# Chunk attention feeding a gated MLP on one core: heads on partition quadrants with runs of 6 or 12 tokens, block transposes in 4-byte words, v as fp32 through the hardware queues, short first blocks

## The chip, the cores and the metric

The program runs on one core of one Trainium2 chip. The metric is the device time of one execution in microseconds (us), and the median over runs is quoted. The profile is of one further execution, taken by the hardware profiler; its times count from the first instruction ("the span").

Engines are named as the profile names them: PE multiplies matrices (PEld is its weight load), DVE is the vector engine, ACT the scalar engine, POOL is GpSimd, SP only issues transfers. Each engine executes its instructions in the order in which the program gives them. Transfers issued from POOL go through the queue that the profile calls software_dynamic; in this kernel they turn fp32 in DRAM into fp16 on the chip on the way. Those issued from SP (and, after the change, from ACT) are called hardware_dynamic and keep the type. All of them pass the core's 16 DMA engines.

## The reference, cut to what matters

```python
# q, k, v: (8, 8, 576, 64) fp32 = batch, heads, sequence, head size
def _attn_ref(q, k, v):                    # chunks of 64 tokens, each attends to itself alone
    q_c = q.reshape(B, H, nc, 64, D)       # k_c and v_c likewise
    scores = scale * np.matmul(q_c, k_c.transpose(0, 1, 2, 4, 3))
    scores = scores - np.max(scores, axis=-1, keepdims=True)
    attn = np.exp(scores)
    attn = attn / (np.sum(attn, axis=-1, keepdims=True) + 1e-09)
    return np.matmul(attn, v_c).reshape(B, H, S, D)

def _moe_ref(x, w_in, w_out, beta):        # x: 4608 tokens x 512; w_in 512 x 2048; w_out 2048 x 512
    h = x @ w_in
    g = h * (1.0 / (1.0 + np.exp(-beta * h)))
    return (g @ w_out).astype(np.float32)

def reference(q, k, v, moe_w_in, moe_w_out, moe_beta):
    attn_out = _attn_ref(q, k, v)
    x = attn_out.transpose(0, 2, 1, 3).reshape(B * S, H * D)
    return _moe_ref(x, moe_w_in, moe_w_out, moe_beta)
```

## The kernel before, in words

All matrix work is in fp16 with fp32 sums. The weights stay on the chip (`w_in16`, `w_out16`). The 4608 tokens pass in 18 units of 256 tokens for the attention, and in 10 blocks for the MLP: two of one unit, then eight of two units (512 tokens).

The attention of a unit has two parts. `emit_sc` (L130) multiplies k by q for all 8 heads of four chunks, 64 small matmuls into two PSUM tiles `sc`, and takes exp on ACT into `et`. `emit_pv` (L149) works on 128 tokens: 16 matmuls of `et` with v and a column of ones give `x` and the row sums; DVE takes the reciprocal (L162) and scales into `x16` (L164); a DMA transpose issued from SP (L169) puts 128 tokens of `xt`, features on partitions, in place for the MLP.

q, k and v come through POOL's queue, converted to fp16 (L87, L95). A partition holds two neighbouring tokens of all heads, so a run of q or k in DRAM is 2 x 64 floats, 512 bytes, and one of v 64 floats, 256 bytes. `emit_T` (L117) then makes the head size the contracted dimension with four DVE transposes per unit in 32x32 blocks of fp16, 512 elements per partition each.

The MLP of a block has two parts. `emit_m(j, m)` (L175) computes 128 of the 2048 hidden features: 4 matmuls into `hps` (L181), tanh on ACT into `sg` (L189), and one DVE instruction for `(sg + 1) * hps` into `gt` (L190; the halves are in `beta2_sb` and in the last scaling). `emit_t(j, t)` (L194) multiplies 128 tokens of `gt` by `w_out16`, 16 matmuls (L197), copies on ACT (L205) and stores from SP (L207).

The order is written out by hand. POOL issues: unit 0, a quarter of w_in, unit 1, the other three quarters, unit 2, four quarters of w_out, unit 3. In block j, between `emit_m(j, 3)` and `emit_m(j, 4)`, stand up to four `emit_t` of block j - 1, each with a step of the attention (for block j + 1) ahead of it. A block's first `emit_m` needs all of its `xt`.

Of the kernel before, what the change touches and what calls it, by code (L numbers as in the profile page):

```python
# [6 lines left out]

FP32 = mybir.dt.float32
FP16 = mybir.dt.float16
ACTF = mybir.ActivationFunctionType  # L10
ALU = mybir.AluOpType
# [3 lines left out]
def kernel(  # L15
# [17 lines left out]
    UNIT = 256  # L33
    NU = NT // UNIT
    NTILE = NT // 128
    VP = 80
# [4 lines left out]
    qk_p = ctx.enter_context(tc.tile_pool(name="qk", bufs=5))  # L41
# [3 lines left out]
    x_p = ctx.enter_context(tc.tile_pool(name="x", bufs=3))  # L45
    gt_p = ctx.enter_context(tc.tile_pool(name="gt", bufs=2))
# [5 lines left out]

    beta_sb = const.tile([128, KFF], FP32)
# [3 lines left out]
    vbig = big.tile([128, NTILE, H, VP], FP16)  # L57

    blocks = []
    u0 = 0  # L60
    for n in [1, 1] + [2] * ((NU - 2) // 2):
        blocks.append((u0, n))
        u0 += n
    NB = len(blocks)
    xt_t = {}
    unit_block = {}
    for j, (u0, n) in enumerate(blocks):
        xt_t[j] = big.tile([128, KDM, n * UNIT], FP16, name=f"xt{j}")
        for u in range(u0, u0 + n):
            unit_block[u] = (j, u - u0)  # L70

    def runs(t0, n):
        done = 0
        while done < n:
            b, s = divmod(t0 + done, S)
            step = min(n - done, S - s)
            yield done, step, b, s
            done += step

    q_t = {}  # L80
    k_t = {}

    def load_qk(u):
        for src, dst, nm in ((q, q_t, "qu"), (k, k_t, "ku")):
            t = qk_p.tile([128, H, 2, D], FP16, tag=nm, name=nm)
            for off, n, b, s in runs(u * UNIT, UNIT):
                nc.gpsimd.dma_start(  # L87
                    out=t[off // 2:(off + n) // 2],
                    in_=src[b, :, s:s + n, :].rearrange("h (p r) d -> p h r d", r=2),
                )  # L90
            dst[u] = t

    def load_v(i):
        for off, n, b, s in runs(i * 128, 128):
            nc.gpsimd.dma_start(  # L95
                out=vbig[off:off + n, i, :, 0:D],
                in_=v[b, :, s:s + n, :].rearrange("h p d -> p h d"),
            )
# [18 lines left out]
    def emit_T(u):  # L117
        for src, dst, nm in ((k_t, kT, "kT"), (q_t, qT, "qT")):
            a = src.pop(u)
            t = qt_p.tile([128, H, 2, 32, 2], FP16, tag=nm, name=nm)  # L120
            for r in range(2):
                nc.vector.transpose(  # L122
                    out=t[:, :, :, :, r],
                    in_=a[:, :, r, :].rearrange("p h (e i) -> p h e i", e=2),
                )
            dst[u] = t

    et_t = {}

    def emit_sc(u):  # L130
        qt, kt = qT.pop(u), kT.pop(u)
        sc = [ps_s.tile([128, H, CH], FP32, tag=f"sc{s}", name=f"sc{s}") for s in range(2)]
        for h in range(H):
            for e in range(2):
                for c in range(4):
                    p0, o0 = 32 * c, 64 * (c % 2)
                    nc.tensor.matmul(  # L137
                        out=sc[c // 2][o0:o0 + 64, h, :],
                        lhsT=kt[p0:p0 + 32, h, e].rearrange("p i r -> p (i r)"),
                        rhs=qt[p0:p0 + 32, h, e].rearrange("p i r -> p (i r)"),  # L140
                        start=(e == 0),
                        stop=(e == 1),
                    )
        for s in range(2):
            et = et_p.tile([128, H, CH], FP16, tag=f"et{s}", name=f"et{s}")
            nc.scalar.activation(out=et, in_=sc[s], func=ACTF.Exp, scale=scale)
            et_t[u, s] = et

    def emit_pv(u, s):  # L149
        i = 2 * u + s  # L150
        et = et_t.pop((u, s))
        x = ps_x.tile([128, 2, 4, 128], FP32, tag="x", name="x")
        for h in range(H):
            for c in range(2):
                p0 = 64 * c
                nc.tensor.matmul(  # L156
                    out=x[p0:p0 + 64, h // 4, h % 4, 0:D + 1],
                    lhsT=et[p0:p0 + 64, h, :],
                    rhs=vbig[p0:p0 + 64, i, h, 0:D + 1],
                )  # L160
        rd = rd_p.tile([128, 2, 4, 1], FP32, tag="rd", name="rd")
        nc.vector.reciprocal(out=rd, in_=x[:, :, :, D:D + 1])  # L162
        x16 = x_p.tile([128, 2, 4, D], FP16, tag="x16", name="x16")
        nc.vector.tensor_tensor(  # L164
            out=x16, in0=x[:, :, :, 0:D], in1=rd.to_broadcast([128, 2, 4, D]), op=ALU.mult
        )
        j, o = unit_block[u]
        t0 = o * UNIT + s * 128
        nc.sync.dma_start_transpose(  # L169
            out=xt_t[j][:, :, t0:t0 + 128], in_=x16.rearrange("p a h d -> p (a h d)")  # L170
        )
# [3 lines left out]
    def emit_m(j, m):  # L175
        n = blocks[j][1] * UNIT
        if m == 0:
            gt_t[j] = gt_p.tile([128, KFF, n], FP16, tag="gt", name="gt")
        hps = ps_p.tile([128, n], FP32, tag="p", name="hps")
        for kk in range(KDM):  # L180
            nc.tensor.matmul(  # L181
                out=hps,
                lhsT=w_in16[:, kk, m * 128:(m + 1) * 128],
                rhs=xt_t[j][:, kk, :],
                start=(kk == 0),
                stop=(kk == KDM - 1),
            )
        sg = sg_p.tile([128, n], FP32, tag="sg", name="sg")
        nc.scalar.activation(out=sg, in_=hps, func=ACTF.Tanh, scale=beta2_sb[:, m:m + 1])  # L189
        nc.vector.scalar_tensor_tensor(  # L190
            out=gt_t[j][:, m, :], in0=sg, scalar=1.0, in1=hps, op0=ALU.add, op1=ALU.mult
        )

    def emit_t(j, t):  # L194
        ops = ps_p.tile([128, DM], FP32, tag="p", name="ops")
        for kk in range(KFF):
            nc.tensor.matmul(  # L197
                out=ops,
                lhsT=gt_t[j][:, kk, t * 128:(t + 1) * 128],
                rhs=w_out16[:, kk, :],  # L200
                start=(kk == 0),
                stop=(kk == KFF - 1),
            )
        osb = osb_p.tile([128, DM], FP32, tag="osb", name="osb")
        nc.scalar.activation(out=osb, in_=ops, func=ACTF.Copy, scale=0.5)  # L205
        r0 = blocks[j][0] * UNIT + t * 128
        nc.sync.dma_start(out=out[r0:r0 + 128, :], in_=osb)  # L207

    attn = [[("sc", 0)], [("pv", 0, 0)]]
    for u in range(NU):  # L210
        attn.append(([("sc", u + 1)] if u + 1 < NU else []) + [("pv", u, 1)])
        if u + 1 < NU:
            attn.append([("pv", u + 1, 0)])
    attn.reverse()
    nxt_T = [0]
    nxt_load = [0]

    def loads_to(u):
        while nxt_load[0] <= min(u, NU - 1):
            w = nxt_load[0]  # L220
            load_qk(w)
            load_v(2 * w)
            load_v(2 * w + 1)
            nxt_load[0] += 1

    def attn_step():
        if not attn:
            return
        for op in attn.pop():
            if op[0] == "sc":  # L230
                emit_sc(op[1])
                if op[1] + 1 < NU:
                    emit_T(op[1] + 1)
                loads_to(op[1] + 4)
            else:
                emit_pv(op[1], op[2])

    with tc.manual_schedule():
        nc.sync.dma_start(out=beta_sb, in_=moe_beta.rearrange("(k p) -> p k", p=128))
        nc.vector.memset(vbig[:, :, :, D:D + 1], 1.0)  # L240
        loads_to(0)
        load_w_in(0)
        loads_to(1)
# [3 lines left out]
        loads_to(2)  # L247
        load_w_out(0)
        load_w_out(1)
        load_w_out(2)  # L250
        load_w_out(3)
        loads_to(3)
        nc.scalar.activation(out=beta2_sb, in_=beta_sb, func=ACTF.Copy, scale=0.5)
        emit_T(0)
        for _ in range(3):
            attn_step()
        pend = []
        for j in range(NB):
            for m in range(KFF):
                if m == 4:  # L260
                    n_a = 4 if j else 2
                    for t in pend:
                        if n_a:
                            attn_step()
                            n_a -= 1
                        emit_t(j - 1, t)
                    pend = []
                if m in (4, 7, 10, 13) and n_a and (m > 4 or j == 0):
                    attn_step()
                    n_a -= 1  # L270
                emit_m(j, m)
            pend = list(range(2 * blocks[j][1]))
# [32 lines left out]
```

The softmax here doesn't subtract the row's maximum and nothing guards it: scores larger than these inputs give would overflow.

## Time and profile before

| | |
|---|---|
| median of 3 runs | 347.1 us (345.27 to 348.63) |
| the profiled execution's own time | 350.12 us |
| its span, first to last instruction | 348.3 us |
| PE busy | 288.9 us, 83% of the span |
| DVE, ACT, POOL busy | 175.7, 144.5, 77.2 us |
| mean granted TensorE clock | 0.968 |
| DMA through POOL's queue | 79360 packets, 18.36 MB |
| DMA through the hardware queues | 26832 packets, 14.17 MB |

Bytes are counted as written, so a packet of q, k, v or weights counts half of what it read. In the page, busy time and clock stand in 40 slices of the span; the chain that ended last is followed back from the last instruction, step by step, to what released it. Waits are given as "who waited for whom". Where PE is busy in nearly all of a stretch, this stretch is PE's; where it isn't, the chain names what it waited for.

### The profile page before, as it was taken

How to read it: one execution, taken by the hardware profiler on the slowest of the kernel's cores; microseconds unless marked ns; L12 is line 12 of the kernel's file. 1: busy time of each engine (PE TensorE's matmuls, PEld its weight loads, DVE VectorE, ACT ScalarE, POOL GpSimd, SP SyncE). 2: the span in 40 equal slices, each digit the busy share in tenths (PEclk: the TensorE clock that was granted, in tenths of full speed). 3: DMA queues.
4: the chain of work that ended last, by engine and by line, in shares of the span. 5: the costliest groups of instructions: out<-in, count | busy, mean ns of one | idle time of the engine just before them, and what ended most of it. 6: DMA issues, size and time to landing. Idle time of an engine off the chain costs nothing.

```text
span 348.3 us, 7008 instructions
## 1 busy us (share of the span) xinstructions
PE 288.9 (83%) x2944; PEld 142.9 (41%) x2944; DVE 175.7 (50%) x305; ACT 144.5 (41%) x234; POOL 77.2 (22%) x100
## 2 busy tenths in 40 slices
PE   0110274983998599999999999999999999999995
PEld 0110263561443245445544444444444444444442
DVE  1413083662649264685377468637745822720700
ACT  1110153361357222752573275257427623732711
POOL 8628286803053035005402100000000000000000
PEclk9999997896799899999999999999999999999999
DMA  9999999999095949909952900420131042002011
GB/s 97 186 178 186 194 158 169 173 181 147 15 150 52 88 78 180 107 10 122 189 48 51 192 31 2 108 77 0 49 98 39 2 98 86 2 30 86 6 60 60
DMA packets 106223, 32.97 MB, mean 95 GB/s; under 512 B 97488, under 2 KB 101584, under 8 KB 106192
## 3 DMA queue, kind: packets, MB, share of 16 engines
q0 software_dynamic: 79360, 18.36, 61.9%
q1 hardware_dynamic: 26832, 14.17, 17.8%
q8 instruction: 23, 0.38, 0.5%
q14 instruction: 8, 0.07, 0.1%
HBM read 36.71 MB, written 9.44 MB: 132 GB/s over the span
## 4 chain that ended last, share of the span: by engine, by line
PE 77%; DMA 14%; DVE 3%; issue 2%; POOL 2%; ACT 1%; ACTq 0%; DVEq 0%; POOLq 0%
PE ops L197 37%; PE hps L181 34%; DMA ku<-in_k_dram 6%; PE x L156 3%; DMA xt_99<-x_362 2%; DMA xt_101<-x_865 2%; DMA xt_100<-x_548 2%; DMA xt_102<-x_1414 2%; DVE qT L122 1%; DVE kT L122 1%; DVE gt L190 1%; POOL qu L87 1%; POOL vbig L95 1%; ACT sg L189 0%; POOL ku L87 0%
## 5 line engine op out<-in xcount | busy, mean ns | idle before, releaser
L190 DVE SCALAR_TENSOR_TENSOR gt<-sg,hps 128x512 f16<-128x512 f32 (+1 forms) x160 | 100.5, 634 | 99.4 <-ACT sg L189 99.1
L189 ACT ACTIVATE sg<-hps,beta_sb 128x512 f32<-128x512 f32 (+1 forms) x160 | 102.4, 645 | 72.8 <-PE hps L181 68.1
L197 PE MATMUL ops<-w_out_97,gt 128*128 128x512 f16 x576 | 129.9, 380 | 0.0
L181 PEld LDWEIGHTS <-w_in_96 128*128 128x128 f16 x640 | 64.7, 102 | 107.0 <-issue 42.4
L197 PEld LDWEIGHTS <-gt 128*128 128x128 f16 x576 | 54.1, 98 | 62.9 <-issue 0.5
L205 ACT ACTIVATE osb<-ops 128x512 f32<-128x512 f32 x36 | 21.5, 597 | 109.9 <-PE ops L197 95.5
L87 POOL DMA_DIRECT2D qu<-in_q_dram x24 | 19.0, 795 | 98.9 <-DVE qT L122 55.7
L95 POOL DMA_DIRECT2D vbig<-in_v_dram x40 | 33.9, 862 | 8.3 <-DMA w_in_96<-in_moe_w_in_dram 5.2
L122 DVE STREAM_TRANSPOSE kT<-ku 128x512 f16<-128x512 f16 x36 | 24.2, 722 | 21.7 <-DMA ku<-in_k_dram 21.7
L181 PE MATMUL hps<-xt_99,w_in_96 128*128 128x256 f16 x64 | 10.0, 323 | 23.1 <-DMA xt_99<-x_362 21.3
L122 DVE STREAM_TRANSPOSE qT<-qu 128x512 f16<-128x512 f16 x36 | 23.4, 699 | 0.0
L162 DVE RECIPROCAL rd<-x 128x8 f32<-128x8 f32 x36 | 7.2, 199 | 32.1 <-PE x L156 32.1
L181 PE MATMUL hps<-xt_101,w_in_96 128*128 128x512 f16 x64 | 17.4, 431 | 5.9 <-issue 5.1
L137 PEld LDWEIGHTS <-kT 32*64 32x64 f16 x1152 | 11.5, 111 | 22.0 <-DVE kT L122 9.1
L87 POOL DMA_DIRECT2D ku<-in_k_dram x24 | 18.9, 789 | 5.8 <-DMA w_out_97<-in_moe_w_out_dram 4.5
L181 PE MATMUL hps<-xt_102,w_in_96 128*128 128x512 f16 x64 | 15.8, 411 | 3.9 <-DMA xt_102<-x_1414 3.9
L181 PE MATMUL hps<-xt_100,w_in_96 128*128 128x256 f16 x64 | 9.5, 309 | 6.2 <-DMA xt_100<-x_548 4.4
L181 PE MATMUL hps<-xt_103,w_in_96 128*128 128x512 f16 x64 | 14.1, 379 | 0.0
L181 PE MATMUL hps<-xt_104,w_in_96 128*128 128x512 f16 x64 | 14.1, 379 | 0.0
L181 PE MATMUL hps<-xt_105,w_in_96 128*128 128x512 f16 x64 | 14.1, 379 | 0.0
L181 PE MATMUL hps<-xt_106,w_in_96 128*128 128x512 f16 x64 | 14.1, 379 | 0.0
L181 PE MATMUL hps<-xt_107,w_in_96 128*128 128x512 f16 x64 | 14.1, 379 | 0.0
(190 smaller groups left out, 124.4 us busy)
## 6 DMA issues: line engine op xcount, KB each, us to landing
out_dram<-osb SPq DMA_DIRECT2D x36, 256.0 KB, 2.0
vbig<-in_v_dram POOLq DMA_DIRECT2D x32, 128.0 KB, 7.4
qu<-in_q_dram POOLq DMA_DIRECT2D x12, 256.0 KB, 6.6
ku<-in_k_dram POOLq DMA_DIRECT2D x12, 256.0 KB, 8.2
w_in_96<-in_moe_w_in_dram POOLq DMA_DIRECT2D x4, 512.0 KB, 12.2
w_out_97<-in_moe_w_out_dram POOLq DMA_DIRECT2D x4, 512.0 KB, 8.8
qu<-in_q_dram POOLq DMA_DIRECT2D x4, 192.0 KB, 4.1
ku<-in_k_dram POOLq DMA_DIRECT2D x4, 192.0 KB, 7.6
```

The costliest lines, as they stand in the source:

```text
L87: nc.gpsimd.dma_start(out=t[off // 2:(off + n) // 2], in_=src[b, :, s:s + n, :].rearrange("h (p r) d -> p h r d", r=2),)
L95: nc.gpsimd.dma_start(out=vbig[off:off + n, i, :, 0:D], in_=v[b, :, s:s + n, :].rearrange("h p d -> p h d"),)
L122: nc.vector.transpose(out=t[:, :, :, :, r], in_=a[:, :, r, :].rearrange("p h (e i) -> p h e i", e=2),)
L137: nc.tensor.matmul(out=sc[c // 2][o0:o0 + 64, h, :], lhsT=kt[p0:p0 + 32, h, e].rearrange("p i r -> p (i r)"), rhs=qt[p0:p0 + 32, h, e].rea ...
L156: nc.tensor.matmul(out=x[p0:p0 + 64, h // 4, h % 4, 0:D + 1], lhsT=et[p0:p0 + 64, h, :], rhs=vbig[p0:p0 + 64, i, h, 0:D + 1],)
L162: nc.vector.reciprocal(out=rd, in_=x[:, :, :, D:D + 1])
L181: nc.tensor.matmul(out=hps, lhsT=w_in16[:, kk, m * 128:(m + 1) * 128], rhs=xt_t[j][:, kk, :], start=(kk == 0), stop=(kk == KDM - 1),)
L189: nc.scalar.activation(out=sg, in_=hps, func=ACTF.Tanh, scale=beta2_sb[:, m:m + 1])
L190: nc.vector.scalar_tensor_tensor(out=gt_t[j][:, m, :], in0=sg, scalar=1.0, in1=hps, op0=ALU.add, op1=ALU.mult)
L197: nc.tensor.matmul(out=ops, lhsT=gt_t[j][:, kk, t * 128:(t + 1) * 128], rhs=w_out16[:, kk, :], start=(kk == 0), stop=(kk == KFF - 1),)
L205: nc.scalar.activation(out=osb, in_=ops, func=ACTF.Copy, scale=0.5)
```

## The change

- **Tiling of the attention.** A group is 3 chunks (192 tokens), 24 groups in all; a unit of loading is 1 or 2 groups. q and k lie with 4 heads on the 4 quarters of the partitions, 32 partitions each, and 6 (one group) or 12 (two groups) neighbouring tokens in a partition: runs of 1536 or 3072 bytes in DRAM. A unit takes two transfers for k and two for q, each of 4 heads.
- **Transposes.** `emit_T` sees pairs of fp16 as one 4-byte word: one DVE transpose for k and one for q per unit, of 384 or 768 words per partition. The scores' operands are then read with a step of two elements. A group takes 48 score matmuls, and exp over 384 columns, twice.
- **v.** It is loaded as fp32 from SP (six transfers for a unit of one group, eight for two groups; for unit 0 half of them from ACT), and cast into a ring of 36 chunks (`vring`), on ACT for units 0 to 2, later on POOL. Two heads share the 128 partitions; `emit_pv` uses all four 64x64 quarters of the array.
- **Start.** q and k of unit 0 come as fp32 from ACT and SP and are cast on ACT and DVE. 14, 2, 3 and 3 matmuls on zeros (`warm`) stand ahead of and between the first steps.
- **Blocks.** The MLP's blocks have 1, 2, 1, 2, 3, then six times 4, then 3 times 128 tokens. For the first 6 pairs of chunks (128 tokens each) `xt` is made by four PE transposes and an ACT copy (`emit_xt`), later by the DMA transpose as before. The first three blocks are ordered by hand, with `emit_t` of blocks 0 and 1 cut in quarters between the `emit_m` of block 2; from block 3 on the attention steps are spread evenly over the block, the last some 10 `emit_m` ahead of its end.
- **Order of the queues.** SP: k of unit 0, half of v of unit 0, `moe_beta`, v of units 1, 2, 3, 4, then stores, transposes and v as the steps come; a step's v is issued ahead of its transpose. POOL: a quarter of w_in, q and k of unit 1, three quarters of w_in, q and k of unit 2, w_out, q and k of unit 3 and so on. ACT: casts of q and v of unit 0, then `beta2_sb`, then the first exp; the cast of v of unit 1 ahead of the second exp, and that of unit 2 ahead of the copy that makes the `xt` of block 1. In both versions every transfer of a kind (hardware or POOL) waits for the one eight before it, since eight semaphores go round.

The diff, cut to its core (`HP` = 4 pairs of heads, `HH` = 2, `HQ` = 4, `GC` = 3, `VR` = 36, `EARLY` = 6):

```diff
+    for n in [1, 2, 1, 2, 3] + [4] * 6 + [3]:        # blocks, in 128 tokens
+        blocks.append((p0, n))
+        p0 += n
...
+    for b in range(B):                                # units, in groups
+        for n in ([1, 1, 1] if b == 0 else [1, 2]):
+            units.append((sum(x[1] for x in units), n))
...
+            t = qk_p.tile([128, HH, w // 32, D], FP16, tag=nm, name=nm)
+            for hh in range(HH):
                 nc.gpsimd.dma_start(
-                    out=t[off // 2:(off + n) // 2],
-                    in_=src[b, :, s:s + n, :].rearrange("h (p r) d -> p h r d", r=2),
+                    out=t[:, hh],
+                    in_=src[b, hh * HQ:(hh + 1) * HQ, s:s + w, :].rearrange(
+                        "h (p r) d -> h p (r d)", p=32
+                    ),
                 )
...
+    def load_qk0():                                   # the same pattern, fp32
+        for src, nm, eng in ((k, "k0f", nc.sync), (q, "q0f", nc.scalar)):
...
+    def cast_qk0(f32):
+        nc.vector.tensor_copy(out=k_t[0], in_=f32["k0f"])
+        nc.scalar.copy(out=q_t[0], in_=f32["q0f"])
...
+    def load_v(n, engines):
+        t = vf_p.tile([128, uc, HP, D], FP32, tag="vf", name="vf")
+        vv = v[b, :, s:s + w, :].rearrange("(g e) (c p) d -> e p c g d", e=2, p=CH)
+        for e in range(2):
+            eng = engines[e % len(engines)]
+            if uc > HP:
+                for g in range(HP):
+                    eng.dma_start(out=t[64 * e:64 * e + 64, :, g], in_=vv[e, :, :, g])
+            else:
+                for c in range(uc):
+                    eng.dma_start(out=t[64 * e:64 * e + 64, c], in_=vv[e, :, c])
...
+    def cast_v(n):
+        op = nc.scalar.copy if n < 3 else nc.gpsimd.tensor_copy
+            op(out=vring[:, c0:c0 + GC, :, 0:D], in_=t[:, o * GC:(o + 1) * GC])
...
-            for r in range(2):
-                nc.vector.transpose(
-                    out=t[:, :, :, :, r],
-                    in_=a[:, :, r, :].rearrange("p h (e i) -> p h e i", e=2),
+            nc.vector.transpose(
+                out=t.bitcast(FP32).rearrange("p h i r o -> p h r (i o)"),
+                in_=a.bitcast(FP32),
+            )
+            dst[n] = t.rearrange("p h i r o -> p h (i r) o")
...
+                        nc.tensor.matmul(
+                            out=sc[hq // 2][o0:o0 + 64, c, hh, :],
+                            lhsT=kt[32 * hq:32 * hq + 32, hh, cs, e],
+                            rhs=qt[32 * hq:32 * hq + 32, hh, cs, e],
...
+            for r, cp in ((0, 0), (1, 1), (0, 1), (1, 0)):
+                nc.tensor.matmul(
+                    out=x[64 * cp:64 * cp + 64, r, hp, 0:D + 1],
+                    lhsT=et_t[g, hp % 2][64 * r:64 * r + 64, cc, hp // 2, :],
+                    rhs=vring[64 * r:64 * r + 64, c % VR, hp, 0:D + 1],
...
+    def emit_xt(i):
+        for kk in range(KDM):
+            nc.tensor.transpose(
+                out=xp[:, kk, :], in_=x16[:, kk * 128:(kk + 1) * 128], identity=ident
+            )
+        nc.scalar.copy(out=xt_t[j][:, :, o * 128:(o + 1) * 128], in_=xp)
+
+    def warm(n):
+        for _ in range(n):
+            nc.tensor.matmul(out=ps, lhsT=zero[:, 0:128], rhs=zero, start=True, stop=True)
...
     def attn_step():
+        if (2 * npv[0] + 3) // GC >= nsc[0] and nsc[0] < NG:
+            n, last = sc_next()
+            v_to(n + 2)
+            if last:
+                T_to(n + 1)
+                cast_to(n + 1)
+                qk_to(n + 3)
+        pv_next()
...
+        qk0 = load_qk0()
+        v_to(0)
         nc.sync.dma_start(out=beta_sb, in_=moe_beta.rearrange("(k p) -> p k", p=128))
+        v_to(1)
...
+        cast_qk0(qk0)
+        cast_to(0)
+        nc.scalar.activation(out=beta2_sb, in_=beta_sb, func=ACTF.Copy, scale=0.5)
+        T_to(0)
+        warm(14)
+        sc_next()
+        warm(2)
+        pv_next()
+        T_to(1)
+        v_to(2)
+        warm(3)
+        emit_xt(0)
+        for m in range(0, 8):
+            emit_m(0, m)
+        cast_to(1)
+        sc_next()
+        for m in range(8, 12):
+            emit_m(0, m)
+        pv_next()
+        for m in range(12, 16):
+            emit_m(0, m)
+        emit_xt(1)
+        pv_next()
+        cast_to(2)
...
+        warm(3)
+        emit_xt(2)
...
+        for g in range(4):
+            emit_t(0, 0, 4 * g, 4 * g + 4)
+            emit_t(1, 0, 4 * g, 4 * g + 4)
+            for m in range(4 * g, 4 * g + 4):
+                emit_m(2, m)
...
+            need = goal - npv[0]                      # from block 3 on
+            span = max(1, len(slots) - 6 - first)
+            for a in range(need):
+                at_ = first + (a * span) // max(1, need)
+                marks[at_] = marks.get(at_, 0) + 1
```

## The prediction, made before the changed kernel was run

> **What bounds the kernel now.** I read the page first, for where PE works and at which clock.
>
> ```profile
> span 348.3 us, 7008 instructions
> ...
> PE 288.9 (83%) x2944; PEld 142.9 (41%) x2944; DVE 175.7 (50%) x305; ACT 144.5 (41%) x234; POOL 77.2 (22%) x100
> ...
> PE   0110274983998599999999999999999999999995
> ...
> DMA  9999999999095949909952900420131042002011
> ```
>
> PE is idle or broken up for the first third, then solid. The DMA engines are the reverse: full for the first 10 slices. The busy time by stage gives the edges:
>
> ```profile
> core 0: us, PE busy (x) PEld busy (x) DVE busy (x) ACT busy (x) POOL busy (x), PEclk, DMA share, GB/s
> 0.00:41.00 41.00, 3.38 (x161) 3.06 (x162) 9.44 (x17) 3.67 (x6) 23.88 (x34) 1.00 1.49 167
> 41.00:60.00 19.00, 12.83 (x167) 9.55 (x168) 10.45 (x24) 8.55 (x19) 12.75 (x17) 0.91 2.02 167
> 60.00:85.00 25.00, 18.21 (x282) 11.48 (x280) 14.31 (x32) 9.95 (x22) 12.16 (x14) 0.84 1.94 170
> 85.00:116.80 31.80, 27.01 (x289) 12.13 (x290) 18.76 (x32) 14.32 (x22) 8.45 (x11) 0.91 0.80 86
> 116.80:344.30 227.50, 227.45 (x2048) 106.65 (x2048) 122.73 (x200) 107.44 (x165) 19.98 (x25) 0.99 0.46 69
> ```
>
> From 116.8 to 344.3 us PE never rests, so only less PE work could help there, and DVE (54% busy) and ACT (47%) are far from binding. Before, PE lacks input. The chain in order of time names what it lacked:
>
> ```profile
> 6.47 8.94 DMA ku<-in_k_dram
> ...
> 16.54 13.03 DMA ku<-in_k_dram
> ...
> 33.04 7.81 DMA xt_99<-x_362
> ...
> 51.45 6.97 DMA xt_100<-x_548
> ...
> 74.37 7.09 DMA xt_101<-x_865
> ...
> 139.09 13.81 PE hps L181 x64
> ...
> 153.27 3.56 PE ops L197 x16
> ```
>
> Loads of k, then DMA transposes at 7 to 8 us that take 2.4 us later on, when the engines are quiet. The two last lines price PE: 216 ns for a 512-column matmul in `emit_m`, 3.56 us for 128 tokens of `emit_t`.
>
> **PE's work, then what is lost.** By rows before: `emit_m` 8 blocks x 13.81 = 110.5; two 256-token blocks at 117 ns a matmul (20 of them in 2.35 us at 51.8, clock up) x 64 = 15.0; `emit_t` 36 x 3.56 = 128.2; `emit_pv` 36 x 0.37 = 13.3; `emit_sc` 18 x 0.64 (gap in the chain between `ops` and `x`) = 11.5. Sum 278.5. From the last matmul to the end are 4.0. So 348.3 - 278.5 - 4.0 = 65.8 us are lost before 116.8, by waits or the halved clock (0.5 at 60.5 to 61.5, for example). That is all the change can win.
>
> **Work after.** `emit_m`: 6 x 13.81 = 82.9; two blocks of 384 columns, 64 matmuls x 162 = 10.4 each; two of 256, 15.0; two of 128 columns, between 59 ns (half of 117) and 102 ns (a mean weight load, L181) each, I take 80: 5.1 a block. Together 128.9. `emit_t` stays at 128.2. Score matmuls stay 1152, now read with a step of two elements: no row shows a step, so between 11.5 and twice that; I take 11.5, since 64 of them pass in 0.64 us though each lasts some 190 ns by its row, so many overlap and none is alone in setting the pace. `emit_pv` keeps 576 matmuls: 13.3. 24 PE transposes at some 100 ns: 2.4. Sum 284.3. The warm-up matmuls run only while PE waits.
>
> On the step the Trainium skill speaks ("SBUF — State Buffer", in the section on the DMA port swizzle): reads within a 16-byte line are at full speed, so fp16 steps up to 8 elements are free. No row here shows it; by it the term is 11.5, without it up to 23.
>
> **Other parts, off PE.** DVE's 72 transposes of 0.71 us (51 us) become 20 of 384 and 14 of 768 words: at the slope of that row about 25 us. Covered: DVE is half idle; if a 4-byte word took twice as long the gain would be nil, and still be covered, except in unit 0 (1 us). exp: 48 of about 0.49 for 36 of 0.60, the same. POOL's casts, 21 of 768 elements, between 0.8 us (ACT's slope) and thrice that; each is due a unit, some 12 us, later, so covered. Fewer packets: q and k go from 36864 to 8704; a 512-byte source packet goes at 700 per us over all engines, a weight packet of 2 KB at 200, which is 360 against 410 GB/s read. v's 36864 packets remain.
>
> **The start, by packets.** In the trace's packet records from 37.5 to 39.5, each half microsecond holds 77 weight packets of POOL and 79 transpose packets of SP: rings with work take turns, one packet each. Prices per packet and engine: weights 80 ns (100 per half us on 16 engines), v 14 ns (570), `beta`'s 4 bytes 10 ns (815), and 60 ns for 1536 bytes at the weights' rate. First packets come 1.1 us after issue from SP (`beta`: 0.75 to 1.83), 1.75 from POOL. Then:
> - k and q of unit 0, 786 KB: there at 4.5 us.
> - v of unit 0: 48 packets per engine on each of two rings, beside POOL: 48 x (14 + 14 + 80) = 5.1, there at 9.6.
> - `beta`, now behind it on SP: 2048 single elements, 128 per engine, 128 x (10 + 75) = 10.9, there at 20.5. `beta2_sb` and so the first exp wait for it on ACT, and behind that exp all of ACT. (w_in is complete at 18.8.)
> - v of units 1 and 2: 192 packets per engine, 136 beside w_out: 136 x 94 = 12.8, the rest 2.5: there at 36.
>
> The first exp at 20.7, `emit_pv` 21.9, `x16` 23, PE transposes, copy: first `emit_m` at 24.7 (41.0 before). ACT then holds the second exp for the cast of v of unit 1 (29.5) and the copy for block 1 for that of unit 2: 36 + 0.8 (cast) + 0.6 (copy): block 1 starts at 37.5. PE has then done block 0 (5.1), two groups (1.0), three pairs (1.1), transposes (0.3): 7.5. Lost: 30.0.
>
> If instead the hardware rings were not slowed, what block 1 needs (0.8 MB of q and k, 1.2 of v, 1.6 of q and k in units 1 and 2, 4.2 of w_in: 7.8 MB) at 380 GB/s takes 20.5 us: block 1 at 25, lost 17.5. I take the 1:1 row, as it is the only one of two queues; both ends stay in the range.
>
> On k and q of unit 0 the Trainium skill speaks against the change. "DMA: Bandwidth & Descriptors", section "Why a DMA increments its semaphore by 16 and not by 1": a transfer uses as many engines as divide the slowest dimension of both sides, up to 16, and hardware queues take the lowest. Here the source's is 4 heads, so these four would share 4 engines: an estimate of 786 KB at a quarter of 410 GB/s, 7.7 us for 1.9. No row of before shows such a transfer. By the rule the sum grows by 6, to 329.
>
> **After the start.** In block 1 ACT needs 16 x 0.476 + 1.0 (exp) + 1.2 (copies), 9.8 us, against PE's 8.7, and the first steps after are short of slack: 2 lost. w_out is in at 33, before its first use at 46. Then block 4: SP has 14 transfers of v (units 6 and 7) at 0.35 (store row: 0.33) and three transposes at 1.2 to issue within block 3, 8.5 us, plus 2.4 to land, against block 3's 10 us of PE: 2 lost at least, 8 if q and k of units 7 and 8 alternate with v and the clock falls; I take 4. From block 5 on the last transpose has 10 `emit_m`, 8.6 us: no loss if a v unit takes 192 x 14 ns = 2.7 us or 6.5 beside q and k. End: 4.0, as before.
>
> **Sum.** 284.3 + 30.0 + 2 + 4 + 4.0 = 324.3 us of span. The profiled execution had 350.12 for 348.3, so 326.1; it was 350.12 against a median of 347.1, factor 0.991: 323.
>
> **Rivals.**
> 1. *The hardware rings are not held back.* For: POOL's ring may not always be full (its first packets came at 3.0, at a quarter of the later rate until 3.9). Against: the 77 to 79 row. Block 1 at 25: 12.5 less, 311.
> 2. *Unit 0 comes late or the operands' step costs.* Before, a load of k of the same size took 8 to 13 us in the chain; 8 us for 2.5 shifts all after it by 6, and the stepped reads add at most 11.5. One or the other: 329 to 335. For: nothing in the trace shows such a transfer or such a read; against: bytes and packets are fewer.
> 3. *v on SP's queue starves the transposes.* SP issues in order, and a unit's v stands ahead of the step's transpose, in the same ring, at 5 block starts (blocks 4 to 8). If fp32 rows cost far more than the 14 ns of v through POOL, each of these starts waits. To lose 24 us, 5 each, a two-group unit must take 8.6 + 5 us less 2.4 to land, some 11, which is 58 ns a packet. From there on the change is slower: 350 at 60 ns. For: 8 transposes took 7 to 8.3 us in the busy start, though only 512 packets; against: DMA share falls to under a half after 120 us, and these packets are not converted.
> 4. *The change is hidden anyway.* Excluded: in the first third PE waits on just these loads.
>
> **How the numbers follow.** Forecast 0.45, rival 1 0.28, rival 2 0.17, rival 3 0.10. The runs shown spread by 1%, so 1% is about what can be told from no change. Rival 3's upper part is slower (0.07), a sliver of it the same (0.02); the rest is faster, 0.91. The range takes rival 1 at its low end less 3 for its own error, and rival 2 at its high end: 308 to 336.
>
> **What would show it.** First `emit_m` near 25 us, `beta` landing at 20, and `emit_m` of block 1 at 37, the wait before it named as v's DMA or its cast; score matmuls still some 0.5 us a group; a gap of 2 to 8 us ahead of block 4 put down to `xt`, none after; PE solid from some 67 us on. `beta` landing by 12 would show rival 1; k and q of unit 0 landing after 8 would show rival 2; gaps at every block start, rival 3. The forecast is wrong if PE's steady part, by the same rows, takes longer than before for the same matmuls.

## The result, and the profile after

The changed kernel takes 367.0 us, the median of 3 runs (364.9 to 371.6), against 347.1. The ratio is 1.055, with a 95% interval of 1.041 to 1.069: slower by 20 us, where 24 us less were forecast. (The ratio leaves out the third run, 371.6 us, which was in a slower state of the chip; the median has it.) The profiled execution has a span of 365.3 us; the prediction's sum was 324.3, so 41.0 us of span have to be found.

The page of the changed kernel: span, busy times, PE and the DMA engines in 40 slices of 9.1 us, and the queues with their packets and bytes.

```profile
span 365.3 us, 7639 instructions
...
PE 299.4 (82%) x3118; PEld 151.6 (42%) x3118; DVE 167.0 (46%) x301; ACT 157.2 (43%) x288; POOL 66.0 (18%) x99
...
PE   6014788697046975999899799999999999999995
...
DMA  6999996126999897959899594594522302201101
...
q1 hardware_dynamic: 61736, 23.02, 37.1%
q0 software_dynamic: 38016, 13.34, 31.3%
q10 hardware_dynamic: 1080, 0.59, 0.7%
```

Two things were not foreseen. PE has a second hole after the start: it works from the fifth slice on, and falls to 0 and 0.4 in the 11th and 12th, 91 to 110 us. And POOL's queue has 38016 packets for 13.34 MB, where q, k and the weights need 12288.

The busy time by stage (columns as in the prediction's second view) shows the hole from 80 us on, the clock falling with it, and that even from 170 to 240 us PE is not full, as it was before from 116.8:

```profile
80.00:100.00 20.00, 8.92 (x240) 6.64 (x239) 9.67 (x18) 7.53 (x17) 7.56 (x11) 0.81 0.94 135
100.00:120.00 20.00, 11.31 (x125) 6.41 (x125) 8.04 (x19) 6.04 (x12) 6.14 (x10) 0.68 1.48 132
170.00:240.00 70.00, 66.24 (x708) 30.53 (x706) 39.22 (x63) 34.66 (x57) 15.25 (x22) 1.00 0.85 111
```

The chain that ended last, in order of time (start, duration, what), up to block 1, which starts at 46.5 us:

```profile
1.94 15.24 DMA q0f<-in_q_dram
...
17.20 0.42 SPq L357
...
17.66 5.29 SPq L146
...
25.23 10.09 DMA vf<-in_v_dram
...
35.34 9.70 DMA vf<-in_v_dram
```

L357 issues `beta`, L146 v. And the same chain up to block 4, which starts at 113.1:

```profile
76.64 0.61 ACT osb L300
...
77.26 0.33 SPq L302
...
80.93 3.66 DMA vf<-in_v_dram
...
87.50 10.81 DMA qu<-in_q_dram
...
98.40 1.54 DVE qT L181
...
100.00 0.69 DVE x_1438 L226
...
100.79 12.19 DMA xt<-x_1438
```

Read upwards: block 4 waits for a DMA transpose; its `x16` stands on DVE behind T of unit 6, which waits for q; this load waits for its place on POOL, behind a cast of v; this v for its place on SP, behind a store; and the store for `osb` of block 1. The timelines of SP and of POOL in the same stretch (start, duration, what, count, then the idle time before and what ended it) show both queues standing:

```profile
66.85 10.74 SPq L302 DMA_DIRECT2D out_dram<-osb  x3
77.64 3.90 SPq L146 DMA_DIRECT2D vf<-in_v_dram  x6
```

```profile
84.74 0.83 POOL L155 CAST vring<-vf 128x768 f16<-128x768 f32 x1 [21.18 <-DMA vf<-in_v_dram]
85.51 1.33 POOL L106 DMA_DIRECT2D ku<-in_k_dram  x2
```

For 10.7 us SP holds three stores that cannot go yet, and v of unit 5 behind them. POOL stands for 21 us at the cast of that v, and the loads of q and k behind the cast have not been issued, while DMA is nearly idle (0.1 and 0.2 in the eighth and ninth slices, 64 to 82 us). When the loads do go out, they land slowly.

To compare runs I cut each span at the first `emit_m` matmul of blocks 1 and 4 (in the trace, the first with 256 and with 384 columns). Times in us; each row is one profiled execution, "32-row loads" is explained with the first experiment. The packet records do not name an engine; the second column follows from packet counts, which e1a and e1c tell.

| run | engines for each q/k load of units 1 to 16 | up to block 1 | block 1 to block 4 | block 4 to end | span |
|---|---|---|---|---|---|
| after | 4 | 46.5 | 66.6 | 252.2 | 365.3 |
| e1a, 32-row loads in unit 0 only | 4 | 41.2 | 68.0 | 251.7 | 360.9 |
| e3, T later | 4 | 44.3 | 68.2 | 251.6 | 364.1 |
| e2, v of unit 5 early | 4 | 44.6 | 59.4 | 250.0 | 354.0 |
| e7, PE transposes for block 4 | 4 | 44.5 | 57.6 | 255.2 | 357.3 |
| order only | 4 | 42.3 | 55.3 | 259.2 | 356.8 |
| e1c, two heads each | 2 | 44.0 | 67.4 | 267.4 | 378.8 |
| e1b, 32-row loads in later units | 16 | 41.5 | 56.6 | 242.9 | 341.0 |
| v through POOL | 16 | 45.2 | 53.4 | 242.6 | 341.2 |
| 32-row loads everywhere, `beta` first | 16 | 37.1 | 56.9 | 243.3 | 337.3 |
| the same, order mended | 16 | 35.6 | 51.3 | 244.5 | 331.4 |
| the same, PE transposes for block 4 | 16 | 35.2 | 53.8 | 242.9 | 331.9 |

### The profile page after: what moved, and what is told of

Its sections match the earlier page's. It is cut to its first block, busy times and chain, and to the rows that moved or that the text cites. A ratio compares the mean times of both kernels' runs of the same rounds, so it can differ in the third digit from the quotient of the medians.

```text
span 365.3 us, 7639 instructions
## 1 busy us (share of the span) xinstructions
PE 299.4 (82%) x3118; PEld 151.6 (42%) x3118; DVE 167.0 (46%) x301; ACT 157.2 (43%) x288; POOL 66.0 (18%) x99
## 3 DMA queue, kind: packets, MB, share of 16 engines
q1 hardware_dynamic: 61736, 23.02, 37.1%
q0 software_dynamic: 38016, 13.34, 31.3%
## 4 chain that ended last, share of the span: by engine, by line
PE 67%; DMA 18%; DVE 6%; SPq 3%; ACT 2%; issue 2%; POOL 0%; ACTq 0%; DVEq 0%; POOLq 0%
PE ops L290 34%; PE hps L270 29%; DMA vf<-in_v_dram 6%; DMA q0f<-in_q_dram 4%; DMA xt<-x_1438 3%; DMA qu<-in_q_dram 3%; SPq L146 3%; PE x L218 2%; DVE qT L181 2%; ACT sg L278 2%; DVE kT L181 2%; DMA xt<-x_1897 1%; DVE gt L279 1%; DVE gt_536 L279 1%; DVE gt_779 L279 0%
## 5 line engine op out<-in xcount | busy, mean ns | idle before, releaser
L270 PE MATMUL hps<-xt,w_in_104 128*128 128x512 f16 (+3 forms) x768 | 140.5, 339 | 29.7 <-DVE gt L279 13.1
L278 ACT ACTIVATE sg<-hps,beta_sb 128x512 f32<-128x512 f32 (+3 forms) x192 | 109.0, 581 | 65.7 <-PE hps L270 49.7
L279 DVE SCALAR_TENSOR_TENSOR gt<-sg,hps 128x512 f16<-128x512 f32 (+2 forms) x144 | 88.4, 627 | 77.5 <-ACT sg L278 74.2
L290 PE MATMUL ops<-w_out_105,gt 128*128 128x512 f16 x512 | 112.9, 379 | 0.0
L155 POOL CAST vring<-vf 128x768 f16<-128x768 f32 x21 | 17.0, 831 | 167.9 <-DMA vf<-in_v_dram 126.1
L200 PEld LDWEIGHTS <-kT 32*64 32x64 f16 x1152 | 11.9, 110 | 24.9 <-DVE kT L181 14.6
L181 DVE STREAM_TRANSPOSE kT<-ku 128x384 f32<-128x384 f32 (+1 forms) x17 | 19.3, 1138 | 6.0 <-DMA ku<-in_k_dram 6.0
L181 DVE STREAM_TRANSPOSE qT<-qu 128x384 f32<-128x384 f32 (+1 forms) x17 | 19.0, 1117 | 2.1 <-DMA qu<-in_q_dram 2.1
L200 PE MATMUL sc_179<-qT,kT 32*64 32x64 f16 x24 | 0.8, 236 | 12.5 <-DVE qT L181 12.5
L257 PE MATMUL wp<-zero 128*128 128x512 f16 x22 | 9.4, 593 | 1.2 <-DVE zero L359 1.2
L290 PE MATMUL ops<-w_out_105,gt_536 128*128 128x512 f16 x32 | 9.4, 433 | 0.0
L279 DVE SCALAR_TENSOR_TENSOR gt_779<-sg,hps 128x128 f16<-128x128 f32 x16 | 4.4, 289 | 8.5 <-ACT sg L278 8.5
L279 DVE SCALAR_TENSOR_TENSOR gt_279<-sg,hps 128x128 f16<-128x128 f32 x16 | 4.3, 287 | 3.8 <-ACT sg L278 2.9
## 6 DMA issues: line engine op xcount, KB each, us to landing
qu<-in_q_dram POOLq DMA_DIRECT2D x14, 192.0 KB, 12.5
```

The source lines that it names most:

```text
L155: op(out=vring[:, c0:c0 + GC, :, 0:D], in_=t[:, o * GC:(o + 1) * GC])
L181: nc.vector.transpose(out=t.bitcast(FP32).rearrange("p h i r o -> p h r (i o)"), in_=a.bitcast(FP32),)
L200: nc.tensor.matmul(out=sc[hq // 2][o0:o0 + 64, c, hh, :], lhsT=kt[32 * hq:32 * hq + 32, hh, cs, e], rhs=qt[32 * hq:32 * hq + 32, hh, cs, e ...
L257: nc.tensor.matmul(out=ps, lhsT=zero[:, 0:128], rhs=zero, start=True, stop=True)
L270: nc.tensor.matmul(out=hps, lhsT=w_in16[:, kk, m * 128:(m + 1) * 128], rhs=xt_t[j][:, kk, :], start=(kk == 0), stop=(kk == KDM - 1),)
L279: nc.vector.scalar_tensor_tensor(out=gt_t[j][:, m, :], in0=sg, scalar=1.0, in1=hps, op0=ALU.add, op1=ALU.mult)
```

## The experiments

All were timed beside the kernel before on the same chip (347.9, 347.9 and 346.7 us there, in the three groups of four). The changed kernel itself was not timed again; its 367.0 stood beside 347.1. The ratios are to the kernel before. The diffs are cut to their core.

**Unit 0 in 32-row loads (e1a).** A transfer of q or k reads 4 heads x 32 rows, with the heads as the slowest dimension of the source. The edit lets each read one quadrant's 32 rows x 2 heads: 4 transfers of 64 packets instead of 2 of 128.

```diff
-            for hh in range(HH):
-                eng.dma_start(out=f32[nm][:, hh],
-                    in_=src[b, hh * HQ:(hh + 1) * HQ, s:s + w, :].rearrange("h (p r) d -> h p (r d)", p=32))
+            by_quarter = src[b].rearrange("(hh hq) s d -> hq hh s d", hq=HQ)
+            for hq in range(HQ):
+                eng.dma_start(out=f32[nm][32 * hq:32 * hq + 32].rearrange("p h r d -> p h (r d)"),
+                    in_=by_quarter[hq, :, s:s + w, :].rearrange("h (p r) d -> p h (r d)", p=32))
```

> Changed kernel with k and q of unit 0 loaded by quarter of the partitions (four transfers of 32 rows each instead of two whose source has 4 heads as its slowest dimension); nothing else. Theory (four-engine transfers delay the start): both land by about 8 us instead of 17.2, the first exp still waits for beta but by about 21 instead of 30.8, block 1 starts near 37 instead of 46.5, and the span falls by 8 to 10 us, to about 356. Rival (the DMA engines are simply full, order and spread do not matter): block 1 moves by less than 3 us and the span by less than 3.

Measured: 364.1 us (361.5 to 365.9), ratio 1.046 (1.039 to 1.053). The mechanism is there, by the landing and by the packets: the last packet of unit 0's q and k ends at 7.9 us instead of 16.8, and never more than 4 (SP) or 5 (ACT) packets of each queue were under way at once in the changed kernel, against 16 and 15 here. The 4-byte packets that a transfer leaves besides its data say the same: ACT's queue, with q of unit 0 and three transfers of v, has 56 in the changed kernel, which is 2 x 4 + 3 x 16, and 112 here, 7 x 16. But only 3 of the expected 8 to 10 us come out, and the intervals of the two ratios overlap: the first exp is at 23.8 (30.9), `beta` being next, and block 1 at 41.2, then held by v of units 1 and 2.

**Later units in 32-row loads (e1b).** The same edit in `load_qk`, on POOL's queue; unit 0 stays as in the changed kernel.

```diff
-            for hh in range(HH):
-                nc.gpsimd.dma_start(out=t[:, hh], in_=src[b, hh * HQ:(hh + 1) * HQ, s:s + w, :]...)
+            for hq in range(HQ):
+                nc.gpsimd.dma_start(out=t[32 * hq:32 * hq + 32]..., in_=by_quarter[hq, :, s:s + w, :]...)
```

> Changed kernel with the q and k of units 1 to 16 loaded by quarter of the partitions, four transfers per tensor instead of two; unit 0 as in the changed kernel. Theory: the 4-byte filler packets of POOL's ring (25728) fall to a few thousand, a load of q or k lands in 4 to 6 us instead of 8 to 12, and the span falls by about 6 us, to 359. Rival (engines full): landing times stay above 8 us and the span within 3 us of 365.

Measured: 342.95 us (339.6 to 346.1), ratio 0.982 (0.976 to 0.987), four times the gain that I expected. This edit alone turns the change from a loss of 20 us into a gain of 5. The start shrinks by 5 us, the stretch from block 1 to block 4 by 10, and the one behind it by 9; the transpose that block 4 waits for takes 4.9 us instead of 12.2. A load of q or k lands 4.3 to 6.5 us after its issue (medians by tensor and size), as expected, instead of 8.6 to 12.5. POOL's queue row of this run:

```profile
q0 software_dynamic: 14464, 13.25, 28.2%
```

The same bytes to 1% in 23552 fewer packets. Those gone are all of 4 bytes (25728 in the changed kernel, 2176 here).

**The same number of transfers, but two heads each (e1c).** e1b changed two things, the slowest dimension and the number of transfers. This run separates them: 4 transfers for each tensor of a unit, of 64 packets as in e1b, whose slowest dimension is 2 heads.

```diff
             for hh in range(HH):
+                for a in range(2):
+                    h0 = hh * HQ + 2 * a
-                nc.gpsimd.dma_start(out=t[:, hh], in_=src[b, hh * HQ:(hh + 1) * HQ, s:s + w, :]...)
+                    nc.gpsimd.dma_start(out=t[64 * a:64 * a + 64, hh], in_=src[b, h0:h0 + 2, s:s + w, :]...)
```

> Against the changed kernel, q and k of units 1 and later go in 4 transfers for each tensor instead of 2, as in the run with the later units alone (342.95), with the same number of packets of the same size, but each transfer reads 2 heads x 32 rows (slowest dimension 2) instead of 32 rows x 2 heads. Theory (the slowest dimension of the source sets how many engines carry a transfer): each now has 2 engines, so no gain: 363 to 385, with POOL's queue carrying some 30000 packets or more, most of them of 4 bytes. Rival (the gain came from the number of transfers, finer pieces that land earlier): 341 to 347.

Measured: 378.9 us (376.8 to 382.4), ratio 1.093 (1.084 to 1.102), 36 us above e1b with as many transfers, data packets and bytes, and 12 above the changed kernel; the loads land after 7.3 to 11.8 us. The number of transfers is refuted, the slowest dimension shown. POOL's queue:

```profile
q0 software_dynamic: 71808, 13.48, 40.5%
```

The 4-byte packets count the idle engines. With 32-row loads there are 16 for each transfer on POOL's queue (2176 for 128 loads and 8 transfers of weights). Take 16 for each away from the changed kernel's 25728 (64 loads and 8 transfers of weights), and 24576 are left, 384 a load: 12 x 32, and 32 of a load's 128 data packets fall to each of four engines. With two heads 59520 less 2176 leave 57344, 448 a load: 14 x 32. Both come out to the packet: 12 or 14 engines got a 4-byte packet for each packet that one of the others carried. What these packets cost beside the lack of engines, no run separates; unit 0's loads on the hardware queues had none and took until 16.8 us all the same.

**v of unit 5 issued together with v of unit 4 (e2)**, ahead of the stores that it stood behind.

```diff
         cast_to(3)
-        v_to(4)
+        v_to(5)
...
         cast_to(4)
-        v_to(5)
```

> Changed kernel with v of unit 5 issued on SP right after v of unit 4, ahead of the stores of blocks 0 to 1, instead of behind three of them. Theory (SP's order holds v of unit 5 until 77.6 us; POOL's cast of it holds q and k of units 6 and 7; their DVE transposes stand ahead of x16 and so of block 4): v of unit 5 is cast by 62 us, q and k of units 6 and 7 issue some 20 us sooner, block 4 starts near 95 instead of 113, span about 350. Rival (engines full): block 4 starts after 108 and the span stays within 4 us of 365.

Measured: 357.5 us (355.8 to 360.1), ratio 1.028 (1.022 to 1.033): 9.5 us less. Block 4 came at 104.0, not 95, and SP's timeline shows what still stood in the way. The next v, of unit 6, now stands behind four stores:

```profile
52.10 5.37 SPq L146 DMA_DIRECT2D vf<-in_v_dram  x6
64.91 15.00 SPq L302 DMA_DIRECT2D out_dram<-osb  x4
80.01 7.13 SPq L143 DMA_DIRECT2D vf<-in_v_dram  x8
```

**T and casts after the P·V part of a step (e3).** In `attn_step`, the transposes, casts and q/k loads that go with the last group of a unit are put after `pv_next()`, so that `x16` goes ahead of them on DVE.

```diff
-            if last:
-                T_to(n + 1)
-                cast_to(n + 1)
-                qk_to(n + 3)
         pv_next()
+        if last:
+            T_to(n + 1)
+            cast_to(n + 1)
+            qk_to(n + 3)
```

> Changed kernel with each attention step's DVE transposes, casts and q, k loads for the next unit emitted after the step's emit_pv instead of before it. Theory (2.9 us of transposes of a two-group unit stand on DVE ahead of reciprocal, x16 and the hps evictions): the gaps in PE near 130, 173 and 206 us shrink, 1 to 2 us each of 7 units, span down by 5 to 9 us to about 358. Rival (the transposes are covered by slack): within 2 us of 365.

Measured: 365.4 us (364.1 to 368.1), ratio 1.051 (1.046 to 1.056), not to be told from the changed kernel. The place of transposes, casts and loads ahead of `x16` is no cause that shows; since all three moved together, and the transposes are as dear here, their price alone was not tested.

**Stores issued by ACT (e5)**, which has just written `osb` itself.

```diff
-        nc.sync.dma_start(out=out[r0:r0 + 128, :], in_=osb)
+        nc.scalar.dma_start(out=out[r0:r0 + 128, :], in_=osb)
```

> Only change against the changed kernel: the 36 stores of emit_t are issued by ACT, which has just written osb, instead of by SP. Theory (SP's in-order queue: v of unit 5 stands behind three stores that wait for osb, 66.85 to 77.6 us, and POOL's cast and four loads of q and k stand behind that v): v of unit 5 goes out with unit 4's, by 60 us; POOL's cast ends its wait of 21 us; block 4 starts at 95 to 102 instead of 113; span 350 to 355. Rival (the DMA engines are simply full from 80 us on, since q and k load four engines only): the loads start earlier but crowd the same engines, block 4 at 108 or later, span 360 to 365.

Measured: 354.9 us (351.9 to 360.2), ratio 1.017 (1.011 to 1.024): 12 us less, as the theory of SP's order has it. In its profiled execution, the longest of its four, v of unit 5 goes out from 54.4 to 59.2 us, and block 4 starts at 100.8. The rival, that the DMA engines are simply full, falls here and again in e1b.

**PE transposes for block 4 (e7).** The pairs 6 to 8 are transposed by PE, as pairs 0 to 5 are, and not by DMA.

```diff
-    EARLY = 6
+    EARLY = 9
...
                 else:
                     emit_m(sl[1], sl[2])
+                for p in [p for p in x_t if p < npv[0] - marks.get(i, 0)]:
+                    emit_xt(p)
```

> Against the changed kernel, the three pairs of block 4 are transposed by PE (12 matmuls and 3 copies on ACT more) instead of by DMA behind v on SP's queue. If the transposes' place behind v on SP is a cause of its own (the rival of the prediction in which v on SP starves the transposes): the wait of 12.2 us for xt before block 4 goes, block 4 starts near 102 instead of 113 and nothing is given back: span 353 to 357. If q and k's late arrival is what counts, block 4 starts near 102 too, but block 5 then waits for the same loads and transposes as before: span 361 to 366.

Measured: 357.1 us (356.1 to 359.1), ratio 1.030 (1.023 to 1.037). Block 4 starts at 102.1, 11 us earlier, as both theories had it; the stretch behind it grows by 3. So most of the 12.2 us that the transpose took, in a ring behind v and on engines that carried q and k, was a cost of its own. The span of 357.3 lies just above the range of the first theory and clear of the second.

**v through POOL (v part undone, on top of e1b).** v goes through POOL's queue, converted to fp16, straight into `vring`; no casts, no v on SP.

```diff
-                    eng.dma_start(out=t[64 * e:64 * e + 64, c], in_=vv[e, :, c])
+                nc.gpsimd.dma_start(
+                    out=vring[64 * e:64 * e + 64, (g0 * GC + c) % VR, :, 0:D], in_=vv[e, :, c])
```

> q and k of later units in transfers of 32 rows, and the part of the change that moved v is undone: v goes through POOL's queue, converted to fp16 on the way, straight into vring, no casts, SP carries no v. Theory (SP's order costs some 10 us here too, but POOL's in-order queue takes v's place, with 113 more transfers of some 0.6 us each to issue, as in the kernel before): within 6 us of 342.95, so 337 to 349, the wait ahead of block 4 then being for q, k or v by POOL. Rival (moving v to the hardware queue was right in itself and saves what it was meant to): slower than 350. Rival (v on SP is the whole of the remaining loss): below 335.

Measured: 344.3 us (341.5 to 346.2), ratio 0.989 (0.985 to 0.994), within 1.3 us of e1b. With 32-row loads and the rest of the order as it was, moving v to SP is worth nothing that shows; it trades one in-order queue for another.

**32-row loads everywhere and `beta` first.** e1a, e1b, and `beta`'s load as SP's first.

```diff
+        nc.sync.dma_start(out=beta_sb, in_=moe_beta.rearrange("(k p) -> p k", p=128))
         qk0 = load_qk0()
         nqk[0] = 1
         v_to(0)
-        nc.sync.dma_start(out=beta_sb, in_=moe_beta.rearrange("(k p) -> p k", p=128))
```

> q and k of all units in transfers of 32 rows (as in the two runs before, now unit 0 and the later ones together), and beta issued first on SP. Theory (unit 0 and beta no longer bind, v of unit 0 beside w_in and v of units 1 and 2 do): k and q of unit 0 there by 8 us, first exp by 19, block 1 at 38 to 41; time 337 to 341, some 2 to 5 us below the run with the later units alone (342.95). Rival (block 1 waits for v of units 1 and 2 in every case): block 1 at 41.5 and time 343 as there.

Measured: 339.4 us (339.0 to 340.3), ratio 0.976 (0.972 to 0.980), 3.6 below e1b. The first exp is at 16.8 us, block 1 at 37.1. `beta`'s 2048 packets of 4 bytes pass between 2 and 4 us.

**The same with v of unit 5 early and stores from ACT.**

> All that helped, together: q and k in transfers of 32 rows for all units, beta first, v of unit 5 issued with that of unit 4, stores from ACT. Theory (the three causes add up: four engines only, SP's order, the start): block 1 by 41, block 4 at 82 to 88, time 322 to 332, which is the 326 span that was forecast for block 4 at 80. Rival (something else holds block 4, v's own rate on one queue or the throttle): block 4 not before 94, time 337 to 342.

Measured: 332.2 us (330.6 to 333.2), ratio 0.955 (0.950 to 0.959). It beats both kernels, the changed one by 35 us, and lies just above the range that I expected. (The block 4 "forecast at 80" in that text was my reading back; the prediction names no such time.) Its page:

```profile
span 331.4 us, 7727 instructions
...
PE 293.1 (88%) x3118; PEld 150.0 (45%) x3118; DVE 165.9 (50%) x301; ACT 156.7 (47%) x288; POOL 90.5 (27%) x163
...
PE   6238897786797899989998999999999999999995
```

The second hole is gone.

**The three edits of order alone**, with q and k still as 4 heads x 32 rows.

> The three edits of order alone (beta first, v of unit 5 with that of unit 4, stores from ACT) with q and k still in transfers of 4 heads x 32 rows. With the same three and 32-row transfers the time was 332.2. Theory (few engines per transfer is a cause of its own, the largest): 347 to 353, 15 to 20 us above it. Rival (once the order is right, the loads have time enough): 332 to 338.

Measured: 356.2 us (355.0 to 358.6), ratio 1.026 (1.019 to 1.032), 24 us above the same order with 32-row loads. More than the 15 to 20 expected; the engines are a cause of their own.

**The best version and PE transposes for block 4.**

> The best version so far (32-row transfers everywhere, beta first, v of unit 5 early, stores from ACT: 332.2) with block 4's three pairs transposed by PE as well. Its profile shows some 5 us of PE's waits for xt. Theory: 1 to 4 us less, 328 to 331. Rival (PE's own transposes, 1.3 us, and the wait for x16 take it back): 332 to 334.

Measured: 333.1 us (330.6 to 333.7), ratio 0.959 (0.952 to 0.965): no gain. PE transposes for block 4 brought 10 us in the changed kernel and bring nothing once loads and order are mended.

## Why the prediction was wrong, point by point

The 41.0 us are 9.0 up to block 1 (46.5 for 37.5) and 32.0 after it. The first `emit_m` came at 34.7 instead of near 25.

**The step that failed most: the rule of the four engines was weighed for unit 0 and forgotten for the other 64 loads.** The text put the rule of the Trainium skill ("DMA: Bandwidth & Descriptors", section "Why a DMA increments its semaphore by 16 and not by 1") against unit 0, priced it at 6 us, and left it out of the sum because no row of before showed such a transfer. But `load_qk` has the same pattern on POOL's queue, in every unit, and its price there was never worked out. The runs agree with the rule (4 instead of 16 four-byte packets for each of unit 0's transfers, 12 x 32 more of them for each load on POOL's queue). The later units' loads cost 24.1 us (367.0 to 342.95), or 24.0 with unit 0's from the other side (356.2 to 332.2). Unit 0's alone cost 3.0, no more than the spread of the runs. The change replaced loads that had the partitions (128, or 96 and 32 across two batches) as their slowest dimension by loads that have 4 heads there, and this outweighs what fewer, larger packets saved: the queue's packets fell to 38016, not to the 12288 that carry data, and those of q and k are carried by a quarter of the engines for each load.

**Unit 0's landing was mis-sized even by the rule.** The rule's estimate, 7.7 us, took four engines for itself. With the rings in turn on each of them, by the prediction's own prices of 60 ns for a packet of q or k and 80 for a weight packet, 64 packets of each ring on each engine take 64 x (60 + 60 + 80) = 12.8 us, an estimate of 14.8 for the landing; measured 16.8. On 16 engines the same sum gives 3.2 us, there at 5.2; e1a measured 7.9, and the prediction's term was 4.5. So the term was too small even without the rule, and two steps that stood side by side in the text belonged together.

**"POOL's casts ... each is due a unit, some 12 us, later, so covered" was false.** A cast takes 0.83 us, the low bound that was given, and 21 of them 17 us. But the cover asked when the cast's result is due, and not what is queued behind the cast while it waits:

```profile
POOL vring L155 <- DMA vf<-in_v_dram: 126.1, 11, 21.2
...
PE hps L270 <- DMA xt<-x_1438: 7.6, 1, 7.6
```

(Who waited for what: us in total, times, the longest.) From unit 5 on, POOL's loads (48 of the 64) are behind the casts, the casts behind v, and v behind SP's stores. Of the stores on SP the prediction has only the price of one issue; what they wait for was never asked. e2 and e5 show this link: 9.5 and 12 us. Once the loads use all engines it is worth 7.2 (339.4 to 332.2).

**v on SP was mis-sized.** 0.35 us for an issue was a store's row; one of v's 256-row transfers takes SP 0.61 us, six of them 3.90. With 0.05 between two, that is some 390 packets per us; the packet records have 815 of 256 bytes from 80 to 82 us, which is 39 ns a packet on 16 engines, not 14. "I take 4" for block 4 stood for 14 transfers and three transposes on SP; at 0.66 each the 14 take 9.2 us instead of 4.9. The stretch from block 1 to block 4 lost far more than that, as its 66.6 us fall to 51.3 when load pattern and order are mended. Rival 3 had this place right and its pattern wrong: no gap at each of five block starts, but a chain that begins at SP's stores.

**"No loss from block 5 on" failed for the same first reason.** With 4 engines the stretch from block 4 on takes 250 to 259 us, with 16 engines 243 to 245, whatever the order; with two, 267. In the changed kernel PE waits there and its clock falls: it is busy 50.7 of the 56.9 us from 113.1 to 170 us, at a granted clock of 0.91. v's place is not the reason: with v through POOL and 16 engines the stretch is 242.6.

**DVE's transposes: a mis-sized term without effect.** 38.3 us in all instead of 25.

```profile
L181 DVE STREAM_TRANSPOSE kT<-ku 128x768 f32<-128x768 f32 x7 | 10.7, 1535 | 6.0 <-DMA ku<-in_k_dram 6.0
...
L181 DVE STREAM_TRANSPOSE kT<-ku 128x384 f32<-128x384 f32 x10 | 8.6, 860 | 0.0
```

The slope between the two forms is 1.76 ns a word. The text called this covered. e3, where moving them changed nothing, agrees, though it does not undo their price.

**What was right.** The stepped reads of the score matmuls cost nothing: at the full clock one starts 8.1 ns after the other in both kernels (64 within 0.51 us before, 48 within 0.38 after). `beta` behind v did hold the first exp, and with it all of ACT, though at 30.9 instead of 20.7: SP could issue it only at 17.2, after 5.9 us of waiting for q of unit 0, and its packets then took until 30.7. v of units 1 and 2 did release block 1, as named. Rival 2's sign came too (q and k of unit 0 after 8 us), but its price, 6 us, did not show: e1a gave back 3. With the load pattern mended, `beta` first and the rest of the order left alone the change gives 339.4 where 323 was forecast; with the order mended, 332.2, inside the range. So the plan of the change was worth what the prediction thought to within some 9 us; the loss is in how its transfers were written and ordered.

**Still open.** These 9 us were not traced to one cause; in the spans they lie after block 1 (331.4 for 324.3, with block 1 at 35.6 for 37.5). Nor was the tail of `beta` in the changed kernel: 1598 of SP's 4-byte packets pass from 20 to 22 us, the others at some 50 to 90 per us until 30.7. In e1b, where only the later units' loads differ, all pass from 15 to 19 us and the first exp is at 19.6, so the tail belongs to those loads. But few engines alone do not make it: e1c, with two engines a load and twice as many transfers, has the first exp at 21.1.

## What to carry to other kernels

Before pricing a transfer by its bytes and packets, read the slowest dimension of both its sides: a layout that gives DMA longer runs can at the same time take away three quarters of its engines, and a rule that speaks against one transfer of a change must be put to all with the same pattern. Where a wait moves to an in-order queue, follow what stands behind it there, through every queue it reaches (here `osb`, SP, v, POOL, q and k, the block), instead of asking when its own result is due. In POOL's queue, far more packets in the page's row than the program's transfers need (38016 for 12288 here) were the sign of loads on few engines.

## What the runs showed of the hardware that was not expected

- A transfer through POOL's queue that uses 4 or 2 engines puts a 4-byte packet on each idle engine for each packet of a busy one: 384 and 448 a transfer by the counts, besides the 16 that every transfer there has. On the hardware queues there are 4 for a transfer of 4 heads and 16 for one of 32 rows, and none per data packet.
- On POOL's queue more than 4 packets of q and k were under way at once (8.4 of the 1536-byte ones on average while any was, 11.9 with 32 rows outermost), which would mean that different transfers take different sets of four; on SP's and ACT's queues unit 0's loads stayed within 4 or 5 (6 in e1b and e1c).
- Issuing a transfer of v holds SP for some 0.61 us, whether of 256 or of 384 rows, almost twice a store's 0.33. So one queue passes transfers of 256 rows at some 390 packets per us; the DMA share was 0.46 from 80 to 82 us.
- 2048 packets of 4 bytes pass in some 2 us with only q of unit 0 beside them (159 packets), and took 13.5 us, from issue to last packet, behind and beside other loads.
